# A ConvNeXt-V2 block on one core: a shorter boundary between its two passes, another block order behind it, and a lead of two expansions in place of six

## The chip, the cores and the metric

The kernel runs on one core of one Trainium2 chip. The metric is the device time of one launch in microseconds. Three runs of the kernel before took 1432.20, 1429.54 and 1432.58 us, median 1432.2 us. One more execution was profiled.

The engines are named as in the profile: PE is the matrix engine (PEld its weight loads), DVE the vector engine, ACT the activation engine, POOL and SP two more that here do little but issue transfers in the second pass. PSUM is the memory that PE writes; it has eight banks of 512 f32 per partition.

## The reference

The input is one image of 512 x 512 pixels with 96 channels in bf16. E is 384 hidden channels.

```python
out = depthwise 3x3 convolution of x with dw
h = _layernorm(out, axis=-1)
h = jnp.einsum('bhwc,ce->bhwe', h, w1)
h = _gelu(h)
gx = jnp.sqrt((h * h).sum(axis=(1, 2), keepdims=True) + 1e-6)
nx = gx / (gx.mean(axis=-1, keepdims=True) + 1e-6)
h = grn_gamma * (h * nx) + grn_beta + h
h = jnp.einsum('bhwe,ec->bhwc', h, w2)
return x + h
```

The sum in `gx` runs over all pixels of the image. Nothing behind it can start before the last pixel's `h` has been squared and summed, which cuts the kernel into two passes.

## The kernel before

**Tiling.** The image is cut into 128 blocks of four rows, 2048 pixels each. A block is handled as four quads (`NQ` = 4, `t` from 0 to 3) of 512 pixels each.

**First pass**, block after block: convolution on PE, layer norm, the normalized block written to DRAM (`yn_dram`) and read back transposed, then the product with w1 and gelu on ACT. The squares are summed in one of two ways, chosen per quad. A channel-major quad (`cm_unit`: three matmuls of 512 columns, one gelu of 128x1536) has each of its three channel groups reduced on DVE (`entry`, tile `bst`). A pixel-major quad (`px_unit`: six shorter matmuls, one gelu) is squared on PE, by twelve matmuls of the quad with itself summed in one PSUM bank (`gram`; `owe_grams` puts them on a list, `gram_next(n)` issues n of the list). `cm_quads(q)` says how many quads of block q are channel-major. `GROUPS` packs the DVE entries in groups of 32 with a group of its own for the last two blocks; `aggregate` reduces a group, `combine` calls it when a group is full.

**What is kept.** For 36 blocks (`whole`) the gelu output is stored in DRAM (`g_dram`) and loaded again in the second pass; for 8 blocks (`HELD`) it stays in SBUF. These 44 need no recomputing (`free`). For the other 84 (`made_q`; the first three, `KEPT`, are blocks 122, 126 and 127, whose normalized input is still in SBUF) the gelu output is recomputed in the second pass, quad by quad: three matmuls with w1 and one gelu. The texts call one such recomputed quad an expansion; there are 84 x 4 = 336. Its output is a tile `gr`, of which three blocks' worth exist (`GRB`).

**The boundary.** After the last block, the kernel issues the owed grams, reduces the last group, works the sums out (`second_moments`, `sums`, `junk` with `dsum`, `ssq`), takes a reciprocal square root by three Newton steps (`gt`, `gr` of 128x3), sums over partitions by one small matmul with `ones_f`, and scales w2 into `W2s`. Two calls of `advance` put six expansions into this stretch: `advance(4, PRE)`, and at its end `advance(LEAD, PRE)` with LEAD = 6.

**Second pass** (`stage_mm2`), blocks in the order of the list `ORDER`, of which n is the index: each block takes four steps (`sub`), one for each quad. A step is twelve matmuls of 96 columns with `W2s` into one of two PSUM banks, which the texts call a product, and a DVE addition of the bias (`o_sb<-PS,B2c`, 128x384). Every second step has one more DVE addition for the residual (`o_sb<-o_sb,xr`, 128x768). All PE, DVE and ACT instructions run in the order in which they are written, by the wrapper `InOrder`.

**Who sets the order.** `ORDER` mixes made and free blocks. After each product, `pace(n, sub)` decides whether the next expansion or expansions are issued on PE:

```python
soon = (n, sub + 2) if sub < NSUB - 1 else (n + 1, 1)
due = sum(1 for v in todo if v < soon or v[0] < n)
even = LEAD + (n * NSUB + sub + 1) * total / (NSUB * NBLK)
advance(max(due, even), n + PRE)
```

`due` counts the quads that the next product needs at the latest; `even` is a straight line from LEAD to LEAD + 336 over the 512 products. An expansion writes three PSUM banks of a pair of such triples (`banks3`, bank 0 to 5); products use banks 6 and 7. Loads are issued ahead by block index: `load_xr` four blocks, `load_yn` seven, `load_g` five, the last held back until the buffer's earlier user is past (`user`).

Of the kernel before, what the change touches and what calls it, by code (L numbers as in the profile page):

```python
# [15 lines left out]
NEWTON_ITERS = 2  # L16
# [41 lines left out]
def kernel(  # L58
# [17 lines left out]
    E = w1.shape[1]  # L76
# [5 lines left out]
    NBLK = H // GR  # L82
# [13 lines left out]
    def is_held(q):  # L96
        return q in HELD

    def is_whole(q):
        return q < TAIL0 and q % 10 in WHOLE or q == TAIL0  # L100

    def after_whole(q):
        return (q - 1) % 10 in WHOLE

    def cm_quads(q):
        if is_whole(q) or is_held(q):
            return NQ
        if q >= TAIL0:
            return 1 if q >= NBLK - 2 else 0
        return 2 if q >= NBLK - 16 or after_whole(q) or q % 10 in (5, 9) else 3  # L110

    whole = [q for q in range(NBLK) if is_whole(q)]
# [41 lines left out]
    w1p = consts.tile([128, E], bf16, name="w1p")  # L154
# [6 lines left out]
    ones_f = consts.tile([128, 128], f32, name="ones_f")  # L161
    B2bc_f = consts.tile([128, C], f32, name="B2bc_f")

    NENT = sum(cm_quads(q) for q in range(NBLK - 2))
    NLAST = cm_quads(NBLK - 2) + cm_quads(NBLK - 1)
    GROUPS = [min(32, NENT - k) for k in range(0, NENT, 32)] + [NLAST]
    NACC = len(GROUPS)
    mom2 = consts.tile([128, NCH, NACC, 2, 3], f32, name="mom2")
    tot2 = consts.tile([128, NACC, NCH], f32, name="tot2")
# [10 lines left out]
    free, rest = HELD[:2], HELD[2:]  # L180
    for i, q in enumerate(whole):
        free.append(q)
        if (i + 1) * len(HELD[2:]) // len(whole) > len(HELD[2:]) - len(rest):
            free.append(rest.pop(0))
    assert not rest
    made_q = KEPT + [q for q in range(NBLK) if not is_whole(q) and not is_held(q) and q not in KEPT]
    ORDER = []
    for i, q in enumerate(made_q):
        ORDER.append(q)
        while len(ORDER) - i - 1 < ((i + 1) * len(free) + len(made_q) // 2) // len(made_q):  # L190
            ORDER.append(free[len(ORDER) - i - 1])
    assert sorted(ORDER) == list(range(NBLK))
    nth_made = {q: n for n, q in enumerate(made_q)}
    SLOTS = [q % NYT for q in KEPT + [NBLK - 5, NBLK - 4, NBLK - 3]]
# [6 lines left out]
    PS = pspool.tile([128, 8, W], f32, name="PS")  # L201
    p2 = ExitStack()
    with ExitStack() as p1:
        pe, dve, act, pool, sp = (InOrder(tc, e) for e in (nc.tensor, nc.vector, nc.scalar, nc.gpsimd, nc.sync))
# [112 lines left out]
        def recompute(q, t):  # L317
            if t == 0:
                grp[q]["g"] = late.gr.tile([128, NQ, NCH, QW], bf16, name="gr")
            cm_unit(grp[q]["g"][:, t], grp[q]["ynt"], t, grp[q]["w1"])  # L320
# [50 lines left out]
        PRE = 5  # L371
        YPRE = 7
        XPRE = 4
        LEAD = 6
        in_order = [q for q in ORDER if is_whole(q)]
        user = {}
        for i, q in enumerate(in_order):
# [6 lines left out]
        def advance(target, upto):  # L384
            while made[0] < total and made[0] < target:
                n, t = todo[made[0]]
                if n >= upto or nth_made[ORDER[n]] >= used[0] + GRB:
                    break
                recompute(ORDER[n], t)
                made[0] += 1  # L390

        def pace(n, sub):
# [4 lines that stand above are left out]
# [18 lines left out]
        for i in range(NI):  # L415
            dve.tensor_copy(out=dwx[:, i], in_=dw9[:, None, chans(i)].to_broadcast([9, GR, 32]))
            pe.matmul(Ud[:, i, :], lhsT=dwx[:, i].rearrange("p q c -> p (q c)"), rhs=ident_b[:9, :9],
                      start=True, stop=True)
# [213 lines left out]
        def stage_turn(k):  # L632
            NT = (BATCHES[k][1] * GR * NG + 31) // 32 * 32
            rt = rtpool.tile([128, NS], bf16, name="rt")
            dve.transpose(out=rt[:, :NT], in_=rns.pop(k)[:, :NT])
            rts[k] = rt
# [45 lines left out]
        bsts = {}  # L682
        ents = {}
        e_ = 0
        for q in range(NBLK):
            if q == NBLK - 2:
                e_ = 32 * (NACC - 1)
            ents[q] = e_
            e_ += cm_quads(q)
        gs = {}  # L690
# [5 lines left out]
        def quarter(b, t):  # L696
            return gs[b][t] if isinstance(gs[b], list) else gs[b][:, t]

        def entry(b, j, m):
            k, e = divmod(ents[b] + m, 32)  # L700
            if k not in bsts:
                bsts[k] = bstpool.tile([128, NCH, 32, 6], f32, name="bst")
            dve.bn_stats(out=bsts[k][:, j, e, :], in_=quarter(b, m)[:, j, :])
# [3 lines left out]
        def mlp_tail(b, get):  # L707
            if b == IN_GH:
                gs[b] = late.gh.tile([128, NQ, NCH, QW], bf16, name="gh")[:]
            elif b > IN_GH:  # L710
                gs[b] = late.gr.tile([128, NQ, NCH, QW], bf16, name="gr")[:]
            elif b in IN_XT:
                gs[b] = g_xt
            elif b == IN_XIN:
                gs[b] = g_xin
            elif not is_held(b):
                while len(sums_only) < 2 * NQ:
                    sums_only.append(ypool.tile([128, NCH, QW], bf16, name="y_bf")[:])
                gs[b] = sums_only[:NQ]
                sums_only.extend(sums_only[:NQ])  # L720
                del sums_only[:NQ]
            else:
                gs[b] = gpool.tile([128, NQ, NCH, QW], bf16, name="g")[:]
            for t in range(NQ):
                cm = t < cm_quads(b)
                (cm_unit if cm else px_unit)(quarter(b, t), ynts[b], t)
                gram_next(12 if len(grams) > 24 else 6)
                if cm:
                    for j in range(NCH):
                        entry(b, j, t)  # L730
                if t == 1:
                    for k in get("turn"):
                        stage_turn(k)
                if t == 2:
                    for b2 in get("stats"):
                        stage_stats(b2)
                if t > cm_quads(b):
                    owe_grams(b, (t - 1) * QC, t * QC)
            for k in get("moments"):
                stage_moments(k)  # L740
            if cm_quads(b) < NQ:
                owe_grams(b, (NQ - 1) * QC, NQ * QC)
            if is_whole(b):
                stores.extend((b, h) for h in range(3))
# [61 lines left out]
        grams = []  # L806

        def gram_next(n):
            for b, c0, j in grams[:n]:
                c = c0 % QC + j * 128  # L810
                v = quarter(b, c0 // QC).rearrange("p j w -> p (j w)")[:, c:c + 128]
                pe.matmul(gram[:, j, :], lhsT=v, rhs=v, start=False, stop=True, skip_group_check=True)
            del grams[:n]

        def owe_grams(b, c0, c1):
            grams.extend((b, c, j) for c in range(c0, c1, E) for j in range(NCH))

        def aggregate(k):
            bst = bsts.pop(k)
            n = 2 * GROUPS[k]  # L820
            v = bst[:].rearrange("p j e (h s) -> p j (e h) s", h=2)[:, :, :n]
            for j in range(NCH):
                dve.bn_stats(out=mom2[:, j, k].rearrange("p h s -> p (h s)"), in_=v[:, j, :, 1])
            dve.tensor_reduce(out=tot2[:, k, :], in_=v[:, :, :, 2], axis=AX.X, op=ALU.add)

        def combine(b):
            for k in sorted(bsts):
                if k < NACC - 1 and (b >= NBLK - 3 or ents[b + 1] >= 32 * (k + 1)):
                    aggregate(k)

        def second_moments(k0, k1):
# [52 lines left out]
        for s in range(last_slot + 1):  # L884
# [77 lines left out]
            else:  # L962
                b = mlp[0]
# [75 lines left out]
            for b in get("combine"):  # L1039
                combine(b)  # L1040
# [14 lines left out]
        while stores:  # L1055
            store_next()
        gsm = p2.enter_context(tc.tile_pool(name="gsm", side="right", bufs=1))
        gram_next(len(grams))
        aggregate(NACC - 1)
        second_moments(0, NACC)  # L1060
        advance(4, PRE)
        sums = gsm.tile([128, NCH], f32, name="sums")
        dve.tensor_reduce(out=sums[:], in_=parts[:].rearrange("p j k h -> p j (k h)"), axis=AX.X, op=ALU.add)
        for j in range(NCH):
            junk = bstpool.tile([128, 128], f32, name="junk")
            dve.scalar_tensor_tensor(out=junk[:], in0=gram[:, j, :], scalar=1.0, in1=ident_f[:],
                                     op0=ALU.mult, op1=ALU.mult, accum_out=dsum[:, j:j + 1])
# [4 lines left out]
        dve.tensor_scalar(out=gi[:], in0=ssq[:].bitcast(i32), scalar1=-0.5, scalar2=float(0x5F3759DF),  # L1072
                                op0=ALU.mult, op1=ALU.add)
        r = gi[:].bitcast(f32)
        for it in range(3):
            t_ = gsm.tile([128, NCH], f32, name=f"gt{it}")
            dve.scalar_tensor_tensor(out=t_[:], in0=r, scalar=-0.5, in1=r, op0=ALU.mult, op1=ALU.mult)
            dve.tensor_tensor(out=t_[:], in0=t_[:], in1=ssq[:], op=ALU.mult)
            rn_ = gsm.tile([128, NCH], f32, name=f"gr{it}")
            dve.scalar_tensor_tensor(out=rn_[:], in0=t_[:], scalar=1.5, in1=r, op0=ALU.add, op1=ALU.mult)  # L1080
            r = rn_[:]
# [17 lines left out]
                                    op0=ALU.mult)  # L1099
        dve.tensor_copy(out=B2c[:], in_=B2bc_f[:])  # L1100

        advance(LEAD, PRE)
    with p2:
        def out_part(q, o_sb, v):
            r0 = q * GR
# [58 lines left out]
```

## Time and profile before

| what | value |
|---|---|
| median of three runs | 1432.2 us |
| the profiled execution, its own time | 1436.17 us |
| span of the profiled execution | 1434.2 us |
| second pass, first product to last DVE addition | 949.67 to 1431.20 us |
| PE busy from 950 to 1421 us | 470.37 of 471 us |
| ACT busy from 950 to 1421 us | 458.59 of 471 us |
| DVE busy from 950 to 1421 us | 404.90 of 471 us |
| PE busy from 900 to 950 us | 37.03 of 50 us |
| mean granted PE clock of the whole span | 0.994 |

The span goes from the first to the last instruction; the execution's own time holds about 2 us more. A busy figure of PE is the time in which at least one matmul was under way; a single matmul of 96 columns is shown with about 206 ns, though in a row one starts every 42 ns. Nearly all instructions bear the line of the wrapper, L36, so they are told apart by tile: `gr<-PS` is an expansion's gelu, `PS<-ynT,w1p` and `PS<-ynT,w1s` its matmuls, `PS<-W2s,g`, `PS<-W2s,gr` and the like are products.

### The profile page before, as it was taken

How to read it: one execution, taken by the hardware profiler on the slowest of the kernel's cores; microseconds unless marked ns; L12 is line 12 of the kernel's file. 1: busy time of each engine (PE TensorE's matmuls, PEld its weight loads, DVE VectorE, ACT ScalarE, POOL GpSimd, SP SyncE). 2: the span in 40 equal slices, each digit the busy share in tenths (PEclk: the TensorE clock that was granted, in tenths of full speed). 3: DMA queues.
4: the chain of work that ended last, by engine and by line, in shares of the span. 5: the costliest groups of instructions: out<-in, count | busy, mean ns of one | idle time of the engine just before them, and what ended most of it. 6: DMA issues, size and time to landing. Idle time of an engine off the chain costs nothing.

```text
span 1434.2 us, 54995 instructions
## 1 busy us (share of the span) xinstructions
PE 1383.6 (96%) x23332; PEld 829.0 (58%) x23332; DVE 1306.3 (91%) x2400; ACT 1380.3 (96%) x1693; POOL 887.8 (62%) x735
## 2 busy tenths in 40 slices
PE   8999999999999999999999997789999999999998
PEld 3445545555555555455545554467777777777776
DVE  8859999999999999999999998988888888888888
ACT  6889989999999999999999999999999999999997
POOL 2559999999998999999999997301111111111110
PEclk9999999999999999999999999999999999999999
DMA  6577899898888899999898987649999999999997
GB/s 194 169 219 222 248 285 274 259 276 271 258 261 251 268 266 272 290 262 268 258 278 270 266 249 221 187 166 411 415 384 412 404 414 398 414 390 392 397 397 279
DMA packets 167565, 423.65 MB, mean 295 GB/s; under 512 B 34166, under 2 KB 83766, under 8 KB 162710
## 3 DMA queue, kind: packets, MB, share of 16 engines
q1 hardware_dynamic: 151652, 314.59, 69.2%
q0 software_dynamic: 15104, 105.39, 18.5%
q8 instruction: 182, 2.98, 0.9%
q14 instruction: 65, 0.53, 0.1%
q10 hardware_dynamic: 562, 0.15, 0.0%
HBM read 262.16 MB, written 157.79 MB: 293 GB/s over the span
## 4 chain that ended last, share of the span: by engine, by line
PE 57%; ACT 19%; DVE 15%; DMA 4%; POOL 2%; issue 2%; SPq 1%; ACTq 0%; POOLq 0%; DVEq 0%
PE PS L36 57%; ACT g L36 14%; DVE bst L36 10%; ACT y_bf L36 4%; DVE xT L36 2%; DMA yn_dram<-yn 2%; DMA g_dram<-g 1%; POOL ysq L36 1%; POOL yn L36 1%; SPq L36 1%; DVE y_bf L36 1%; DVE o_sb L36 1%; DMA xin<-in_x_dram 0%; DVE mom L36 0%; ACT ysq L36 0%
## 5 line engine op out<-in xcount | busy, mean ns | idle before, releaser
L36 ACT ACTIVATE g<-PS 128x512 bf16<-128x512 f32 (+2 forms) x1160 | 704.1, 780 | 8.4 <-PE PS L36 8.1
L36 DVE BATCH_NORM_STATS2 bst<-g 128x6 f32<-128x512 bf16 x1020 | 622.5, 673 | 20.7 <-ACT g L36 20.4
L36 ACT ACTIVATE gr<-PS 128x1536 bf16<-128x1536 f32 x344 | 479.6, 1456 | 14.0 <-PE PS L36 7.8
L36 POOL TENSOR_TENSOR yn<-y_bf,rbc 128x1536 bf16<-128x1536 bf16 x126 | 391.4, 3108 | 61.6 <-ACT rbc L36 23.8
L36 PE MATMUL PS<-ynT,w1p 128*128 128x512 bf16 x1110 | 344.4, 383 | 19.4 <-ACT g L36 9.3
L36 PE MATMUL PS<-xT,Wq 64*32 64x511 bf16 (+1 forms) x9198 | 337.9, 387 | 7.4 <-ACT y_bf L36 0.8
L36 DVE TENSOR_TENSOR o_sb<-PS,B2c 128x384 bf16<-128x384 f32 x512 | 280.0, 555 | 58.4 <-PE PS L36 52.9
L36 POOL TENSOR_TENSOR ysq<-y_bf 128x1536 bf16<-128x1536 bf16 x114 | 313.3, 2748 | 26.0 <-ACT y_bf L36 20.0
L36 PEld LDWEIGHTS <-g 128*128 128x128 bf16 (+1 forms) x3603 | 218.3, 98 | 121.5 <-issue 39.6
L36 PE MATMUL PS<-ynT,w1s 128*128 128x512 bf16 x972 | 262.7, 379 | 0.0
L295 POOL DMA_DIRECT2D xr<-in_x_dram x116 | 62.2, 537 | 286.2 <-DVE o_sb L36 286.2
L36 PEld LDWEIGHTS <-gr 128*128 128x128 bf16 x4104 | 201.0, 98 | 53.8 <-issue 0.7
L36 PE MATMUL PS<-W2s,gr 128*128 128x96 bf16 x4032 | 209.8, 206 | 1.0 <-DVE o_sb L36 0.4
L36 ACT ACTIVATE y_bf<-PS 128x1536 bf16<-128x1536 f32 (+2 forms) x147 | 182.5, 1263 | 13.8 <-PE PS L36 13.2
L36 DVE STREAM_TRANSPOSE xT<-xin 128x576 f32<-128x576 f32 (+1 forms) x256 | 181.6, 749 | 11.0 <-PE PS L36 7.0
L36 PEld LDWEIGHTS <-w1p 128*128 128x128 bf16 x1110 | 95.5, 98 | 162.1 <-issue 114.3
L36 PEld LDWEIGHTS <-Wq 64*32 64x32 bf16 x9216 | 104.9, 90 | 127.4 <-ACT g L36 56.8
L36 PE MATMUL PS<-g 128*128 128x128 bf16 x1632 | 159.0, 220 | 6.4 <-DVE PS L36 5.8
L36 DVE TENSOR_TENSOR o_sb<-o_sb,xr 128x768 bf16<-128x768 bf16 x256 | 142.7, 557 | 8.9
L36 PE MATMUL PS<-w1p,ynT 128*128 128x384 bf16 (+1 forms) x924 | 141.6, 273 | 7.0 <-ACT y_bf L36 2.0
L36 PEld LDWEIGHTS <-ynT 128*128 128x128 bf16 x924 | 73.0, 97 | 59.1 <-issue 36.7
L36 PE MATMUL PS<-W2s,g 128*128 128x96 bf16 x1968 | 103.8, 206 | 0.2
(114 smaller groups left out, 660.3 us busy)
## 6 DMA issues: line engine op xcount, KB each, us to landing
g<-g_dram POOLq DMA_DIRECT2D x36, 1536.0 KB, 9.6
xin<-in_x_dram SPq DMA_DIRECT2D x126, 432.0 KB
g_dram<-g SPq DMA_DIRECT2D x105, 512.0 KB
yn_dram<-yn SPq DMA_DIRECT2D x512, 96.0 KB
ynT<-yn_dram SPq DMA_DIRECT2D x128, 384.0 KB
out_dram<-o_sb SPq DMA_DIRECT2D x127, 384.0 KB
xr<-in_x_dram POOLq DMA_DIRECT2D x124, 384.0 KB, 7.4
ynT<-yn_dram SPq DMA_DIRECT2D x243, 128.0 KB
```

The costliest lines, as they stand in the source:

```text
L36: r = f(*a, **k)
L295: pq.dma_start(out=xr[:], in_=x[0, r0:r0 + GR].rearrange("r w c -> (r w) c").rearrange("(p g) c -> p g c", g=PXP))
```

## The change

Seven edits, all at or behind the end of the first pass:

1. `cm_quads` gives 0 in place of 1 for the last block, so that its four quads are all pixel-major and only block 126 still sends three entries to DVE. The separate last group of entries goes away: all entries are packed in one sequence, and `combine` takes each group when it is full or the last block is done.
2. During the last two blocks up to 12 grams are issued per quad, not 6.
3. In the boundary, the last reductions come ahead of the last grams, `advance(1)` ahead of both, `advance(3)`, `advance(4)` and, at the end, `advance(5)` behind them.
4. Four matmuls of 384 columns into PSUM bank 6 that nobody reads are issued between the third and the fourth expansion.
5. Two Newton steps (`NEWTON_ITERS` is 2), not three.
6. The first two held blocks (116 and 117) go to the very front of `ORDER`; the other 42 free blocks are spread between the made ones by another formula.
7. LEAD in `pace` is 2, not 6.

```diff
@@ cm_quads
-            return 1 if q >= NBLK - 2 else 0
+            return 1 if q == NBLK - 2 else 0
@@ groups
-    NENT = sum(cm_quads(q) for q in range(NBLK - 2))
-    NLAST = cm_quads(NBLK - 2) + cm_quads(NBLK - 1)
-    GROUPS = [min(32, NENT - k) for k in range(0, NENT, 32)] + [NLAST]
+    NENT = sum(cm_quads(q) for q in range(NBLK))
+    GROUPS = [min(32, NENT - k) for k in range(0, NENT, 32)]
@@ order of the second pass
+    lead, free = free[:2], free[2:]
...
-        while len(ORDER) - i - 1 < ((i + 1) * len(free) + len(made_q) // 2) // len(made_q):
+        while len(ORDER) - i - 1 < i * len(free) // (len(made_q) - 1):
             ORDER.append(free[len(ORDER) - i - 1])
+    ORDER = lead + ORDER
...
-        LEAD = 6
+        LEAD = 2
@@ mlp_tail
-                gram_next(12 if len(grams) > 24 else 6)
+                gram_next(12 if len(grams) > 24 or b >= NBLK - 2 else 6)
@@ combine
-                if k < NACC - 1 and (b >= NBLK - 3 or ents[b + 1] >= 32 * (k + 1)):
+                if b == NBLK - 1 or ents[b + 1] >= 32 * (k + 1):
                     aggregate(k)
@@ boundary
-        gram_next(len(grams))
-        aggregate(NACC - 1)
+        advance(1, PRE)
         second_moments(0, NACC)
-        advance(4, PRE)
         sums = gsm.tile([128, NCH], f32, name="sums")
         dve.tensor_reduce(out=sums[:], ...)
+        gram_next(len(grams))
+        advance(3, PRE)
+        for k in range(4):
+            pe.matmul(PS[:, 6, :E], lhsT=w1p[:, :128], rhs=w1p[:], start=True, stop=True)
+        advance(4, PRE)
         for j in range(NCH):
             junk = ...
...
-        for it in range(3):
+        for it in range(NEWTON_ITERS):
...
-        advance(LEAD, PRE)
+        advance(5, PRE)
```

In the built program this gives, with m for a made block and f for a free one, the sequence `m f m m f m m f ...` before (with one `m f m f` about every 32 blocks) and `f f m m m f m m f m m f ... m m f m f` after.

## The prediction

> **What bounds the kernel now.** I read the chain of waits first, then the stage table, then the timeline at three places. The chain over the last 480 us is PE almost alone, and the stage table says why:
>
> ```profile
> core 0: us, PE busy (x) PEld busy (x) DVE busy (x) ACT busy (x) POOL busy (x), PEclk, DMA share, GB/s
> 950.00:1421.00 471.00, 470.37 (x6984) 352.11 (x6981) 404.90 (x749) 458.59 (x330) 85.19 (x159) 1.00 0.99 394
> ```
>
> In the second pass PE never waits (470.37 of 471 us), and ACT, with one gelu per expansion, is nearly as full. So PE has no slack there: each wait of PE that the change brings is added to the time. The steady rhythm, and the last expansion:
>
> ```profile
> 1419.25 0.81 PE L36 MATMUL PS<-ynT,w1s 128*128 128x512 bf16 x3
> ...
> 1419.90 0.67 PE L36 MATMUL PS<-W2s,g 128*128 128x96 bf16 x12
> ...
> 1420.41 0.81 PE L36 MATMUL PS<-ynT,w1s 128*128 128x512 bf16 x3
> ...
> 1421.06 1.18 PE L36 MATMUL PS<-W2s,gr 128*128 128x96 bf16 x24
> ...
> 1422.08 0.81 PE L36 MATMUL PS<-ynT,w1s 128*128 128x512 bf16 x3
> ...
> 1430.64 0.56 DVE L36 TENSOR_TENSOR o_sb<-o_sb,xr 128x768 bf16<-128x768 bf16 x1
> ```
>
> The starts give PE's prices: an expansion 0.65 us (1419.25 to 1419.90), a product 0.51 (1419.90 to 1420.41). The last expansion is at 1422.08, and ten products stand behind it, which DVE paces. Then the boundary:
>
> ```profile
> 941.97 0.84 PE L36 MATMUL PS<-gr 128*128 128x128 bf16 x12 [0.20 <-ACT gr L36]
> ...
> 942.65 1.46 PE L36 MATMUL PS<-ynT,w1p 128*128 128x512 bf16 x6
> ...
> 943.50 17.89 ACT L36 ACTIVATE gr<-PS 128x1536 bf16<-128x1536 f32 x13 [1.58 <-PE PS L36]
> ...
> 944.25 0.28 DVE L36 SCALAR_TENSOR_TENSOR junk<-PS,ident_f 128x128 f32<-128x128 f32 x1
> ...
> 946.57 0.16 DVE L36 SCALAR_TENSOR_TENSOR gt<-gr 128x3 f32<-128x3 f32 x1
> ...
> 947.38 0.38 PE L36 MATMUL PS<-rs__21840,ones_f 128*128 128x1 f32 x2 [0.23 <-DVE gx L36]
> ...
> 949.03 0.81 PE L36 MATMUL PS<-ynT,w1p 128*128 128x512 bf16 x3 [0.54 <-ACT gr L36]
> ...
> 949.67 0.67 PE L36 MATMUL PS<-W2s,gr 128*128 128x96 bf16 x12
> ```
>
> These lines also hold a price that the steady pass hides, the way from an expansion to the product that reads it. The expansion of 942.65 is taken up by ACT at 943.50, 0.85 later. A gelu lasts 1.45 us (median of the 344 in the view of the tile gr). ACT's previous work ended at 941.92, and PE, which waited for it, went on at 941.97: 0.05. So a product can start 0.85 + 1.45 + 0.05 = 2.35 us after its expansion starts, 1.70 after PE has left the expansion. In the kernel before, five to eleven other products stand between (the first four quads apart), and nobody sees these 1.70 us.
>
> **The boundary (edits 1 to 5).** Before, DVE reduced six entries from 938.83 to 942.49, aggregated them and came to `junk` at 944.25. Three entries of 0.61 us and one aggregation of three reductions and `tot` (0.36, 942.40 to 942.76) go away: DVE would be there at 944.25 - 1.8 - 0.4 = 942.0. But `junk` reads the gram bank, and the last quad's twelve grams now stand behind the last gelu, whose end at 941.92 nothing moves: grams from 941.97 to 942.65, their result at about 942.9 (each takes 0.22). So the wait moves from DVE to ACT and PE, and the gain here is 1.35 us. The third Newton step is three instructions 0.197 apart (946.57 to 947.16): 0.6. The first product was behind the expansion at 949.03, which waited for a bank; one expansion fewer stands there: 0.3. Together the first product starts 2.3 us earlier, at about 947.4. The twelve extra grams (0.68) and the four unread products (0.64, four of 384 columns at 0.16) lie in PE's waits of this stretch: PE was busy 37.03 of 50 us there. If they did not fit they would cost at most 1.3. The twelve grams per quad in the last two blocks fit: 0.65 + 0.68 is within ACT's 1.34 per gelu, as the pair 935.25 and 936.59 shows. One expansion fewer is ahead of the products, so PE has one more behind them: +0.65. Held blocks first moves one load of `g` ahead of one `xr` on POOL; a load lands 9.6 us after issue and is needed some five blocks of 3.7 us later, so nothing waits; SP's reads of `ynT`, seven blocks ahead, are covered in the same way.
>
> **The order and the lead (edits 6 and 7).** This is where the sum is decided. Behind the two held blocks the order needs 8 expansions in every 3 blocks, 2.667 a block. The straight line of `pace` grants 336/128 = 2.625. At block 2 the line stands at 2 + 2 x 2.625 = 7.25 quads with none needed, a good lead; each block takes 0.042 of it, and at block 126 it is 2.0. A pair of made blocks uses eight quads while the line grants 5.25, so 2.75 are lent within each pair, and from about block 70 on the line is too late: `due` takes over, and `due` issues a quad right in front of its product. Before, the line matched the order's average and started six ahead, so the lead never ran down.
>
> I walked `pace` through both orders; the built program has PE's instructions in the same sequence, and its products wait for the gelu of their own quad. Of the 336 quads of the changed kernel, this many have so much between expansion and product: nothing, 72; one product, 22; one product and one expansion, 20; two products and one expansion, 42. The 72 lie late: 3 in blocks 64 to 79, 13 in 80 to 95, 23 in 96 to 111, 33 in 112 to 127. Per quad PE waits:
>
> - nothing between: 1.70 us, 72 x 1.70 = 122
> - one product: at most 1.70 - 0.51 = 1.19; the product between is often itself late, which leaves less, so I take 0.9: 22 x 0.9 = 20
> - a product and an expansion: at most 1.70 - 0.51 - 0.65 = 0.54; I take 0.45: 20 x 0.45 = 9
> - two products and an expansion: about 0.1: 42 x 0.1 = 4
>
> That is 155 us. ACT does not hide it: it waits for PE in the same alternation. Nor is it won back, since `pace` counts products, not time. A quad that comes late also leaves free blocks without expansions: twelve runs of three to five products, where before there was one, the tail. DVE needs (4 x 0.534 + 2 x 0.557)/4 = 0.81 us a product, PE 0.51, so those beyond the second wait for a bank, some 0.7 a run, 8 us; the shorter tail, five products in place of ten, gives back about 3. Net +5.
>
> **Sum:** -2.3 + 0.65 + 155 + 5 = +158 us. Made on the profiled span it is 1434.2 + 158 = 1592; that execution took 1436.17, some 4 us over the median shown, so for the median I take 1432.2 + 158 = 1590.
>
> **Bounds.** If each product also shows its first weight load (98 ns in the group of weight loads `<-gr`, hidden before), the 156 delayed quads give +15. If the three kinds with something between wait half as long as taken, it is -16. So 1574 to 1605. The unread products at their most are in that.
>
> **Rivals.** *The clock falls in the late half.* These rows are PE's clock around a short gap:
>
> ```profile
> 863.00:864.00 1.00, 0.00 (x0) 0.00 (x0) 0.33 (x1) 1.00 (x3) 1.00 (x1) 1.00 0.17 16
> ...
> 866.00:867.00 1.00, 1.00 (x5) 0.40 (x4) 0.14 (x1) 1.00 (x1) 1.00 (x1) 0.50 0.72 168
> ```
>
> A gap of 1.75 us, behind some short matmuls, cost half the clock for about 3.4 us; gaps of 2.65 us (to 181.78) and 2.09 (to 30.37) did too. Against it: from 944 to 948, with matmuls in about 40% of the time by their starts, the clock stayed at 1.00. The late alternation is 1.16 us of matmuls in 2.86, also 40%, right between. At half clock it takes about 4 us, so 3.4 us at half clock lose 1 us; every second such stretch in the 220 to 250 us of the alternation gives some 30: 1620. The Trainium skill (TensorE: Matmul & The Clock Gate, HAM oscillation) puts the limit at idle gaps over about 3.4 us; by that no gap here would do it and 1590 would stand. The rows disagree with that, as 1.75 us was enough.
>
> *Part of the wait is covered.* If PE's wait were only that of the quads with nothing between, and at the rate of half a gelu, 72 x 0.85 = 61, it would be 1432.2 + 61 + 3 = 1497. Against it: PE runs in order and the product's first weight load waits; there is nothing else it could run.
>
> *Faster: only boundary and tail count.* If the expansions' 2.35 us stayed hidden, the change would be -2.3 + 0.65 and about -1.5 from the five products fewer in the tail: 1429. This holds as long as the lead stays above two quads to the end. For it speaks that the first 60 blocks do keep it; against it that the line ends at 2.0 and each pair needs 2.75. It would need the products to be issued elsewhere than counted.
>
> **How the numbers follow.** Forecast 1590: 62%. Clock: 27%. Partly covered: 6%. Faster: 4%; no change, 1%. The range takes the forecast's own bounds and the clock case with some margin: 1565 to 1628. A difference within 0.2% (3 us) can't be told from none; faster 0.04, same 0.01, slower 0.95.
>
> **What would show it.** In the changed trace: PE waits `<-ACT gr` of about 1.7 us in the second pass, none before block 45, and densest at the end; PE busy about as in 950 to 1421 at first and near half at the end; stretches of 16 blocks that take 60 us at first and some 125 at the end; the first product near 947.4; `junk` at 942.9 released by PE; the clock at 1.00 in the late half (forecast) or in part 0.50 (rival). If the second half runs at the pace of the first, the prediction is wrong.

## The result, and the profile after

| | before | after |
|---|---|---|
| median of the runs | 1431.72 us (4 runs, 1429.54 to 1432.58) | 1655.89 us (4 runs, 1650.96 to 1657.42) |
| profiled span | 1434.2 us | 1654.1 us |
| last gelu of the first pass to the first product | 7.76 us | 5.07 us |
| first product to last DVE addition | 481.5 us | 700.2 us |
| mean granted PE clock | 0.994 | 0.937 |

The change makes the kernel 15.4% slower: ratio 1.1539, 95% interval 1.1508 to 1.1571. That is 224 us, where 158 were forecast, and it lies over the top of the predicted range (1628).

The stage table of the changed kernel shows where. Its columns are span, busy time of PE, PEld, DVE, ACT and POOL, then PE's granted clock, the share of the DMA engines and GB/s:

```profile
950.00:1010.00 60.00, 59.25 (x888) 44.69 (x888) 51.70 (x101) 56.26 (x42) 11.28 (x21) 1.00 0.92 366
...
1160.00:1240.00 80.00, 74.28 (x1056) 52.25 (x1052) 62.19 (x115) 69.47 (x50) 12.90 (x24) 1.00 0.96 366
1240.00:1320.00 80.00, 62.18 (x799) 41.90 (x797) 47.19 (x87) 54.62 (x40) 9.69 (x18) 0.93 0.80 277
1320.00:1400.00 80.00, 56.90 (x655) 38.30 (x656) 37.69 (x69) 43.52 (x31) 8.60 (x16) 0.84 0.67 234
1400.00:1480.00 80.00, 55.15 (x510) 34.41 (x507) 30.50 (x56) 34.40 (x24) 5.91 (x11) 0.67 0.48 161
1480.00:1560.00 80.00, 50.40 (x494) 31.82 (x494) 28.82 (x53) 34.49 (x24) 6.45 (x12) 0.73 0.53 178
1560.00:1640.00 80.00, 50.38 (x457) 31.88 (x456) 26.39 (x49) 29.02 (x20) 3.23 (x6) 0.65 0.24 84
```

The first 240 us of the second pass run as before. Then every engine thins out together: PE, ACT, DVE and the transfers all lose, so none of them has become the bound. And the clock, which the forecast held at 1.00, falls to about two thirds. The waits view names the pair that holds each other up (engine and what it waited for; total us, times, longest):

```profile
ACT gr L36 <- PE PS L36: 220.4, 122, 5.4
PEld L36 <- ACT gr L36: 202.8, 135, 2.5
PE PS L36 <- ACT gr L36: 135.2, 118, 1.6
```

In the timeline both parts of the loss can be read, first an alternation of one expansion and its own product at half clock, then one at the full clock:

```profile
1505.56 1.48 PE L36 MATMUL PS<-ynT,w1s 128*128 128x512 bf16 x3
...
1507.07 1.45 ACT L36 ACTIVATE gr<-PS 128x1536 bf16<-128x1536 f32 x1 [2.51 <-PE PS L36]
1508.58 1.14 PE L36 MATMUL PS<-W2s,gr 128*128 128x96 bf16 x12 [1.54 <-ACT gr L36]
1509.52 1.48 PE L36 MATMUL PS<-ynT,w1s 128*128 128x512 bf16 x3
...
1521.22 0.81 PE L36 MATMUL PS<-ynT,w1s 128*128 128x512 bf16 x3
...
1522.07 1.45 ACT L36 ACTIVATE gr<-PS 128x1536 bf16<-128x1536 f32 x1 [1.42 <-PE PS L36]
1523.57 0.68 PE L36 MATMUL PS<-W2s,gr 128*128 128x96 bf16 x12 [1.54 <-ACT gr L36]
1524.09 0.81 PE L36 MATMUL PS<-ynT,w1s 128*128 128x512 bf16 x3
```

At full clock the alternation lasts 2.87 us (1521.22 to 1524.09), where the same two took 1.16 before; the parts are 0.85 to the gelu's start, 1.45 of gelu, 0.05 to the product, 0.52 of product. At half clock it lasts 3.96 (1505.56 to 1509.52). The boundary did what was said, and somewhat more:

```profile
945.11 1.55 PE L36 MATMUL PS<-gr 128*128 128x128 bf16 x24
...
946.69 0.29 DVE L36 SCALAR_TENSOR_TENSOR junk<-PS,ident_f 128x128 f32<-128x128 f32 x1 [0.61 <-PE PS L36]
...
949.02 0.16 DVE L36 SCALAR_TENSOR_TENSOR gx<-ssq,gr 128x3 f32<-128x3 f32 x1
...
950.82 1.33 PE L36 MATMUL PS<-W2s,g 128*128 128x96 bf16 x24
```

These times are later than those of before since this execution's first pass took 3.8 us longer (its last gelu ends at 945.75, not 941.92). The bracket behind `junk` shows the moved wait: DVE now waits 0.61 us for the grams on PE.

### The profile page after: what moved, and what is told of

Its sections match the earlier page's. It is cut to its first block, busy times and chain, and to the rows that moved or that the text cites. A ratio compares the mean times of both kernels' runs of the same rounds, so it can differ in the third digit from the quotient of the medians.

```text
span 1654.1 us, 55023 instructions
## 1 busy us (share of the span) xinstructions
PE 1467.0 (89%) x23351; PEld 861.4 (52%) x23351; DVE 1307.6 (79%) x2390; ACT 1385.7 (84%) x1693; POOL 889.0 (54%) x735
## 4 chain that ended last, share of the span: by engine, by line
PE 49%; ACT 26%; DVE 13%; DMA 7%; issue 2%; SPq 1%; POOL 1%; ACTq 0%; POOLq 0%; DVEq 0%
PE PS L36 49%; ACT g L36 11%; ACT gr L36 10%; DVE bst L36 8%; ACT y_bf L36 3%; DMA xin<-in_x_dram 3%; DVE xT L36 3%; DMA rbc<-r_dram 2%; DMA yn_dram<-yn 2%; SPq L36 1%; DMA ynT<-yn_dram 1%; DVE o_sb L36 1%; DVE y_bf L36 1%; ACT xT L36 0%; POOL yn L36 0%
## 5 line engine op out<-in xcount | busy, mean ns | idle before, releaser
L36 ACT ACTIVATE gr<-PS 128x1536 bf16<-128x1536 f32 x344 | 485.2, 1457 | 225.1 <-PE PS L36 220.4
L36 PE MATMUL PS<-W2s,gr 128*128 128x96 bf16 x4032 | 238.7, 216 | 133.9 <-ACT gr L36 133.5
L36 PEld LDWEIGHTS <-gr 128*128 128x128 bf16 x4116 | 213.0, 103 | 234.6 <-ACT gr L36 202.8
L36 PEld LDWEIGHTS <-g 128*128 128x128 bf16 (+1 forms) x3603 | 231.8, 103 | 123.2 <-issue 49.1
L36 PE MATMUL PS<-ynT,w1s 128*128 128x512 bf16 x972 | 290.1, 411 | 0.0
L36 PE MATMUL PS<-W2s,g 128*128 128x96 bf16 x1968 | 118.4, 221 | 0.7 <-DVE o_sb L36 0.4
L36 PEld LDWEIGHTS <-w1s 128*128 128x128 bf16 x972 | 83.1, 104 | 45.0 <-issue 11.8
```

The costliest lines, as they stand in the source:

```text
L36: r = f(*a, **k)
```

## The experiments

What had to be told apart: whether edit 7 (the lead) or edit 6 (the order) does the harm; whether the 66 us beyond the forecast are the clock's or come from waits priced too low; what the clock goes by; and what the boundary is worth. Changes are shown against the changed kernel, unless the kernel before is named. Behind most ratios stands the time from the end of the first pass's last gelu to the last DVE addition, taken from single records of the trace ("second part"; 489.3 us before, 705.3 after), since the end of that gelu wandered between 936.3 and 951.9 us from one execution to the next.

**lead6.** `LEAD = 6` in place of 2.

> Undoes edit 7 alone: LEAD is 6 again in pace, everything else as changed. Theory A (the line of pace runs out of lead, so that expansions stand right in front of their products): with 6 the line still has about 6 quads at block 126 and at least three products stand between each expansion and its product, so no PE waits for gr in the second pass are left, the clock stays at 1.00, and the time is that of the kernel before less the boundary's gain: 1430 us, ratio to before 0.997 to 1.000. Rival B (the new order of blocks itself is what costs, by its held blocks first or by the pairs of made blocks): the time stays far over before, 1500 us or more, with waits for gr in the late half.

Measured: 1436.62 us, ratio 1.0026 (1.0010 to 1.0041); clock 0.994; second part 489.0 us. The loss is gone with this one number, so rival B falls, and the clock is back over the second pass:

```profile
950.00:1435.00 485.00, 480.57 (x7143) 360.10 (x7141) 415.99 (x776) 464.81 (x334) 85.40 (x159) 1.00 0.97 386
```

But theory A said 1430 us, below the time of before, and the launches are 0.26% above it. Of the 2.69 us that the boundary gains, 2.4 are given back within the first 16 blocks, which take 63.0 us and not 60.6; see boundary_only and no_unread.

**lead2_old_order.** The kernel before with the lead of two:

```diff
-            even = LEAD + (n * NSUB + sub + 1) * total / (NSUB * NBLK)
+            even = 2 + (n * NSUB + sub + 1) * total / (NSUB * NBLK)
```

> The kernel before with 2 in place of 6 in the line of pace alone; boundary, order and the six expansions of the boundary stay. In the old order the line has the slope of the order, so the lead is short all along the pass and not only late: 65 quads have nothing between expansion and product and 83 one product. Theory A: at 1.70 us and up to 1.2 us a quad some 170 us at full clock, and more with the clock at one half in parts, so 1600 to 1670 us, spread over the whole pass. Rival B (it is the new order): within 1% of before, 1420 to 1446 us.

Measured: 1647.79 us, ratio 1.1498 (1.1464 to 1.1532). As theory A has it, the loss is much the same in size but lies all along the pass: the eight stretches of 16 blocks took 71, 98, 74, 106, 74, 98, 74 and 104 us (before: 58 to 61), and the clock fell in the long ones, as in these two windows:

```profile
1050.00:1150.00 100.00, 80.53 (x1014) 55.27 (x1012) 58.83 (x109) 65.67 (x47) 12.34 (x23) 0.90 0.72 257
1150.00:1250.00 100.00, 79.19 (x964) 53.47 (x964) 56.61 (x104) 64.51 (x46) 11.81 (x22) 0.86 0.76 271
```

**lead4.** `LEAD = 4`.

> The changed kernel with LEAD 4: the line ends at 4.0 quads at block 126. Of the 336 quads 2 have nothing between expansion and product, 12 one product, 23 two. Theory A: 2 x 1.70 and 12 x about 0.9, some 13 us of waits, and a pass too full for the clock to fall: 1442 us (1437 to 1450). Rival (any lead under six costs in proportion to what is missing, 224 us for four): 1540 us.

Measured: 1447.89 us, ratio 1.0108 (1.0086 to 1.0131); second part 500.8 us, 11.5 over before. This is within theory A's band, though the clock did fall once, for 3.4 us at 1429 us. The loss is not in proportion to the lead: 6, 4 and 2 give 1437, 1448 and 1656 us. It goes with the count of quads that have too little between expansion and product.

**fill24.** Unread products in PE's waits, into columns of a bank that nothing else uses:

```diff
             advance(max(due, even), n + PRE)
+            nxt = (n, sub + 1) if sub < NSUB - 1 else (n + 1, 0)
+            if made[0] and todo[made[0] - 1] == nxt:
+                for k in range(24):
+                    pe.matmul(PS[:, 6, E:W], lhsT=w1p[:, :128], rhs=w1p[:, :128], start=True, stop=True)
```

> The changed kernel with 24 unread products of 128 columns (1.37 us by the grams' 0.057 us each) issued on PE wherever the next product's own quad was issued just before, into 128 columns of PSUM bank 6 that nothing else uses: they fill PE's wait of 1.70 us and make it no longer. Theory A (the clock falls because PE's matmuls fill only 40% of the late half): the clock stays at 1.00 in the second pass, the waits for the gelu remain, and the time falls to what the waits alone cost, 1590 us (1575 to 1605). Rival (the part beyond the forecast comes from something else than the clock, such as transfers or DVE): no faster than the changed kernel, 1650 us or more, with the clock at 1.00.

Measured: 1613.26 us, ratio 1.1261 (1.1240 to 1.1281); clock 0.997. More work on PE made the kernel 43 us faster, with the clock up, but the time is over the band that the theory gave. The timeline shows why:

```profile
1566.31 0.67 PE L36 MATMUL PS<-W2s,g 128*128 128x96 bf16 x12
1567.63 1.50 PE L36 MATMUL PS<-w1p 128*128 128x128 bf16 x24 [0.65 <-DVE o_sb L36]
1568.96 0.67 PE L36 MATMUL PS<-W2s,gr 128*128 128x96 bf16 x12
```

The expansion was at 1565.66; its product, due at 1565.66 + 2.35 = 1568.0, came at 1568.96, behind a filler that had waited for DVE. The experiment itself was at fault: the filler also stood where a product and not an expansion came before it.

**fillb22.** The same with 22, and only where this call of `advance` issued an expansion (`made[0] > was`, with `was` taken ahead of it).

> As fill24, but 22 unread products of 128 columns (1.25 us) only at the 72 places where an expansion was issued just now and its own product comes next. In fill24 they also stood behind products with no expansion before them (M 1566.31, filler 1567.63 to 1568.96), where the wait was shorter than the filler and grew. Theory A: the clock stays at 1.00 in the whole second pass and no wait grows, so the time is the forecast's, 1590 us (1580 to 1600): the waits cost 158 us and the clock the other 65. Rival (the waits themselves were priced too low, and the filler of fill24 cost nothing): 1610 us or more.

Measured: 1593.35 us, ratio 1.1122 (1.1095 to 1.1150); clock 0.996, and 1.00 all through the second pass. Second part 649.3 us, 160.0 over before, against 158 in the forecast.

```profile
1400.00:1480.00 80.00, 70.43 (x1021) 53.08 (x1019) 36.55 (x68) 41.45 (x30) 7.50 (x14) 1.00 0.58 195
1480.00:1560.00 80.00, 69.63 (x1010) 53.69 (x1008) 30.65 (x57) 36.85 (x27) 5.90 (x11) 1.00 0.48 163
```

The single terms agree too. If the starts in this trace are lined up with the order in which `pace` issues the work, PE's delays (beyond 0.65 us for the expansion or 0.51 for the product ahead) add up to 123 us before the 72 products with nothing between, to 20, 8 and 4 us for the three other kinds of quads, and to 9 us before the products of free blocks (forecast: 122, 20, 9, 4 and 8). So the waits were priced right, and the other 56 us of the second part (705.3 - 649.3) are the clock's: compared product by product, the changed kernel loses 55.8 us to fillb22 between products that touch its stretches at half clock, and nothing (-0.1 us) between all others.

**fillb4, fillb1.** The same with 4 and with 1.

> The same with 4 unread products (0.23 us) at each of the 72 places, so that matmuls fill (0.65 + 0.51 + 0.23)/2.87 = 48% of the late alternation instead of 40%. If the clock falls below a share somewhere between 40 and 48%, it stays at 1.00 nearly throughout and the time is 1590 to 1600 us; if the share must be higher, or if it is the length of a gap that counts (1.5 us here, 1.7 without), it goes on falling and the time is 1620 to 1655 us.

> One unread product of 128 columns (0.057 us) at each of the 72 places, so that matmuls fill some 42% of the late alternation where four filled 48% and none 40%. If the clock falls below a share close to 40%, it falls less often than in the changed kernel and the time lies between, 1600 to 1640 us; if the share is nearer 48%, it is as in the changed kernel, 1645 to 1660 us.

Measured: 4 fillers: 1595.41 us, ratio 1.1137 (1.1100 to 1.1174), clock 0.997. 1 filler: 1647.31 us, ratio 1.1494 (1.1455 to 1.1533), clock 0.949, 154 us of the second part at half clock where the changed kernel has 195. First fillb4, then fillb1, in the stage table:

```profile
1400.00:1480.00 80.00, 51.98 (x691) 34.93 (x692) 35.44 (x66) 41.48 (x30) 7.52 (x14) 1.00 0.58 200
1480.00:1560.00 80.00, 48.18 (x630) 32.39 (x628) 31.27 (x58) 37.29 (x26) 6.45 (x12) 1.00 0.52 174
```

```profile
1400.00:1480.00 80.00, 56.57 (x595) 36.94 (x593) 34.28 (x63) 37.36 (x27) 7.50 (x14) 0.77 0.52 173
1480.00:1560.00 80.00, 52.71 (x503) 34.37 (x503) 28.07 (x52) 32.14 (x23) 5.36 (x10) 0.72 0.50 171
```

Four products of 0.057 us in each of 72 places are worth 60 us of the launch; fillb4's second part is that of fillb22 (649.3 us). The share of the alternation in which PE's matmuls run, by their starts, is 40% with none, 42% with one, 48% with four; the clock falls in the first two and holds in the third.

**fillnarrow.** As fillb22, with 24 unread products of 4 columns (`PS[:, 6, E:E + 4]`, `rhs=w1p[:, :4]`).

> 24 unread products of 4 columns each at the 72 places. In the first pass twelve such short products take 0.30 us, so 24 fill some 0.6 us of each wait of 1.70 and leave a gap of 1.1 us, shorter than fillb4's 1.5; but they stream only 24 x 4 columns, a fifth of what fillb4's four products of 128 do. If the clock goes by the length of PE's gaps or by how long PE has instructions, it stays at 1.00 and the time is 1590 to 1597 us as in fillb4. If it goes by the columns streamed, it falls as in fillb1 and the time is 1635 to 1660 us.

Measured: 1655.04 us, ratio 1.1553 (1.1492 to 1.1613); clock 0.937, as if nothing had been filled in.

```profile
1522.23 0.81 PE L36 MATMUL PS<-ynT,w1s 128*128 128x512 bf16 x3
1523.05 0.74 PE L36 MATMUL PS<-w1p 128*128 128x4 bf16 x24
1524.65 0.69 PE L36 MATMUL PS<-W2s,gr 128*128 128x96 bf16 x12 [0.86 <-ACT gr L36]
```

```profile
1320.00:1400.00 80.00, 64.15 (x915) 46.15 (x913) 35.64 (x66) 41.91 (x30) 7.75 (x15) 0.79 0.64 223
1400.00:1480.00 80.00, 63.94 (x862) 46.58 (x861) 29.68 (x55) 34.71 (x25) 5.89 (x11) 0.67 0.48 159
```

PE idles 0.79 to 0.98 us in front of these 72 products, less than the 1.16 to 1.32 that fillb4 leaves, so in each alternation it is busy for longer. It is also busier in the same windows (63.94 of 80 us against 51.98), though there the half clock itself stretches its matmuls. Yet the clock falls. So neither the length of the gap nor PE's busy figure is what counts; of the three readings only the columns streamed agree.

A count over all traces is sharper. In each trace the clock's falls start on one grid with a step of 3.41 us. Cut the second passes of all 14 profiles into the stretches of that grid, and count in each the columns that PE streams, at 0.216 us per 512 columns (a start every 0.216 us in the expansions) and twice that at half clock. Of the stretches at full clock, the 58 behind which the clock fell are streamed for 33.2 to 36.4% of their time, and the 2109 behind which it held for 36.6% or more. From half to full clock it came behind 54 stretches with at least 79%, and it stayed at half behind 143 with at most 78%. A stretch of 3.41 us can hold one alternation's matmuls and waits on both sides of them. By the same prices that is an estimate of 33% with no filler, 35% with one, 40% with four, and 34% with the 24 narrow ones. If each narrow one is counted by the 0.026 us from start to start, the stretches before fillnarrow's falls come to 52 to 70% and the others to 54% or more, and nothing parts them. The limit is read from the second pass alone: in the first pass, whose matmuls have other shapes, one fall (at 876 us in no_unread) came behind a stretch of about 38%.

**boundary_only.** Edits 1 to 5; order and LEAD as before.

> Edits 1 to 5 alone: the changed boundary, with the old order of blocks and LEAD 6. By the changed kernel's trace the first product comes 5.06 us behind the end of the first pass's last gelu, 2.69 sooner than before (7.75). One expansion more is left for the second pass (0.65). Theory: 2.0 us faster than before, 1429.7 us, ratio 0.9975 to 0.9995. Rival (what is gained at the boundary is given back in the second pass, since its first products wait for the expansions that are missing): within 0.5 us of before.

Measured: 1434.55 us, ratio 1.0011 (0.9995 to 1.0027): no gain, where the theory had 2.0 us. Of the 2.69 us, 1.35 are given back at once: one more expansion (0.65), and one that waits 0.7 us for a bank behind the first product. Some 5 us more that this profile's second part lost (493.3 us) lie in four single waits of 0.8 to 1.9 us in mid-pass, which no other profile here shows at these places; two of the four end with a read of `ynT`.

**order_only.** The kernel before with edit 6 alone.

> The kernel before with the new order of blocks alone (edit 6), its boundary, six expansions and LEAD 6 kept. Theory: the new order by itself costs nothing that can be measured, within 0.2% of before, and behind the first pass's last gelu it takes about what lead6 takes plus the 2.7 us of the boundary, 492 to 496 us (before: 492.3). Rival (held blocks first leave ACT and PE idle at the start): 498 us or more behind that gelu, ratio 1.004 or more.

Measured: 1432.57 us, ratio 0.9996 (0.9982 to 1.0010); second part 492.9 us. In the launch time the new order by itself costs nothing that can be measured. The second part of this one profile is 3.7 us longer than before's, all in the first 16 blocks; 2.2 us of it are two waits of PE for reads of `ynT`, which the profiles of lead6 and of the changed kernel do not have.

**no_unread.** lead6 without the four unread products (edit 4).

> lead6 without the four unread products of the boundary (edit 4). If they hold the clock up, it falls to 0.50 for 3.4 us or more within 10 us of the boundary and the second pass is 1 to 3 us longer than in lead6 (492.05 us behind the last gelu of the first pass); if PE's other work there suffices, clock and time are as in lead6 within 0.5 us.

Measured: 1436.47 us, ratio 1.0020 (0.9998 to 1.0042). Its second part is that of lead6 to the hundredth (489.02 us), with the clock at 1.00 throughout: edit 4 does nothing here. Its profiled first pass ended at 951.9 us, lead6's at 946.3; so differences of some us between launches of such kernels are made in the first pass. They are not made by edits 1 and 2, since the last 16 gelus of the first pass, where these act, take 32.2 us in every profile here. What makes them stays open.

**slope6.** LEAD 6 with a line that has the slope of the new order:

```diff
-            even = LEAD + (n * NSUB + sub + 1) * total / (NSUB * NBLK)
+            even = LEAD + max(0, (n - 2) * NSUB + sub + 1) * total / (NSUB * (NBLK - 2))
```

> The changed kernel with LEAD 6 and a line that follows the new order: even = 6 + (products behind block 2) x 336/504, so the lead neither runs out (LEAD 2) nor shrinks from 11 to 6 (LEAD 6). At least three products stand between each expansion and its product. Theory A (only the lead matters, and with it in hand the boundary's 2.7 us are kept less one expansion): 2 to 4 us faster than before, 1429 us, ratio 0.997 to 0.9995. Rival (the boundary's gain is given back at the start of the second pass, as lead6 and boundary_only suggest): within 2 us of before, ratio 0.9985 to 1.003.

Measured: 1433.11 us, ratio 1.0004 (0.9984 to 1.0024). Its second part is the shortest of all, 486.0 us, 3.3 under before, with PE busy for 465.00 of the 465 us from 955 to 1420. But the launches spread from 1426.2 to 1440.9 us, and over them nothing of it can be told from no change, so the time lies in the rival's band. No version here is measurably faster than the kernel before.

## Why the prediction was right or wrong

**The mechanism was right.** `LEAD` alone brings the loss and takes it away (lead6), it works in the old order too (lead2_old_order), and at full clock the waits come out as summed, in total (160.0 us against 158) and term by term (fillb22). The eight stretches of 16 blocks in fillb22 took 59, 60, 60, 62, 74, 90, 110 and 127 us; the prediction named 60 at first and some 125 at the end. The way from an expansion to its product was 2.35 us as read from the boundary of the kernel before.

**The step that failed is the clock.** The prediction took the clock at 1.00 into the forecast and kept its fall as a rival with 27% and a price of 30 us. It fell. Both the choice and the size were off. The choice rested on one stretch (944 to 948) with about 40% of matmuls at full clock, held against three short gaps with a fall; one stretch of 4 us was no ground for 200 us of the same share. By the count under fillnarrow, the stretch of the clock's grid that lies there, 943.80 to 947.22, was streamed for 42%, above the 36.4% up to which the clock fell; the alternation comes down to 33% in the stretches that hold a single one. The size took falls of 3.4 us in every second stretch of the alternation, some 30 losses of 1 us. In the trace there are 15 falls of 3.4 to 23.9 us, 195 us of the second part in all and more than half of what lies behind 1320. Only one of the 15 ended after 3.4 us: an alternation at half clock is streamed for 57% of its 3.96 us, below the 79% at which the clock came back. It takes 3.96 us for 2.87, so 195 x (1 - 2.87/3.96) = 54 us, against 56 between the changed kernel and fillb22.

The Trainium skill (TensorE: Matmul & The Clock Gate, HAM oscillation) has the clock fall at idle gaps over about 3.4 us. By that it would have held, and 1590 would have been the time. In the second pass the changed kernel's gaps are at most 1.6 us and the clock fell, so here the measurement decides against the rule as stated in that section.

**The other steps.** The boundary: 2.69 us measured for 2.3 predicted, with `junk` 0.94 us behind the last gelu (0.98 predicted) and released by PE. The unread products cost nothing, as said (no_unread); the extra grams were not tried alone, but `junk` came as early as forecast with them in place. What was not said is that one expansion then waits 0.7 us for a bank, which with the one expansion more halves the gain. Held blocks first and the earlier load of `g` cost nothing in the launch time (order_only), though the reads of `ynT`, taken to be covered, were waited for in two profiles, 2.2 us each. The rival of partly covered waits and the faster one both fell: from block 64 on the lead was short, as counted.

## What to carry to other kernels

How many units an order needs and how many its pacing grants must be compared as slopes, not as totals: 2.667 against 2.625 a block looks like nothing and uses up five quads in 126 blocks. Where a consumer is issued right behind its producer on another engine, price the whole way through that engine and back (here 2.35 us for 0.65 of work), once for each place that the order shows. And a PE that waits often can also run slower: look at the share of time in which columns stream, in the emptiest stretch of 3.41 us and not on average, and not at the busy figure, and test it with a few unread products in the waits, which cost nothing if they fit.

## What was not expected of the hardware

PE's clock stood at half for 195 us of the second part though no wait of PE was longer than 1.6 us. It held at 1.00 with 48% of the alternation in streaming matmuls and fell at 42% and 40%; counted in stretches of the clock's own grid of 3.41 us, it fell behind those with 33.2 to 36.4% and held behind those with 36.6% or more. It came back only behind stretches with 79% or more. Matmuls of 4 columns did not count for it: 24 of them in each wait raised PE's busy time in one 80 us window from 55 to 64 us and left the launch at 1655.0 us, while four of 128 columns brought it to 1595.4.
